# The first weights in eight transfers, two x tiles on ScalarE's queue, and another order at the end

## The chip, the cores and the metric

The kernel runs on one core of a Trainium2 chip. The metric is the time of one execution on the device in microseconds (us). The engines of the core are named as in the profile: PE is the matmul engine (TensorE), PEld its weight load, DVE is VectorE, ACT is ScalarE, POOL is GpSimd, SP is SyncE, which here only issues transfers (DMAs). Each engine works through its own instructions in the order in which they stand, and waits on semaphores for the others.

## What is computed

The input x is 2048 rows of 512 in bf16. The layer norm of it, xn, goes two ways, and the two meet at the end.

```python
def reference(A_x, A_wqkv, A_wo, B_x, B_w1, B_w2, B_w3, B_w4):
    x = A_x
    xn = _layernorm(x)
    s = _A_ref(xn, A_wqkv, A_wo)                      # 32 heads of 16, 8 keys at distance 2
    g = _silu(_B_ref(xn, B_w1, B_w2, B_w3, B_w4))     # mixer with shifts, then an MLP of 1376
    return x + s * g
# _A_ref: q, k, v = xn @ wqkv; each row i attends to rows i, i-2, .. i-14; softmax; o @ wo
# _B_ref: h = gelu(_layernorm(xn) @ w1); the four quarters of h are shifted by +1, -1, +2, -2 rows;
#         x1 = xn + h_shifted @ w2; x1 + gelu(_layernorm(x1) @ w3) @ w4
```

## The kernel before

Even and odd rows are kept apart (parity p = 0, 1), since attention at distance 2 never mixes them. Each parity is 1024 rows, held as eight tiles of 128 rows; four tiles are a chunk, so there are chunks 0 to 3. Rows lie on the partitions in the tiles `xn`, and the transposes `xnT` feed the projections.

**The start.** SP issues, in this order: x tiles 0 and 1 (128 KB each), the query half of the weights `wqk_sb` (512 KB in one transfer), x tiles 2 and 3, the key half, then the x tiles of chunks 1 and 2 in pairs, `w1_sb`, and chunk 3. Meanwhile PE runs ten warming matmuls on ones (`warm_ps`). For chunk 0, `stats` (DVE, L208 and L209) makes mean and variance of one tile, `root` (ACT, L217) the square root, `inverse` (DVE, L220) and `norm` (DVE, L224) the normalised tile. `first_columns` transposes tiles 0 and 1 on PE (L290) and copies the result out in halves, one on DVE (L292) and one on ACT (L293). Then `qk(0, 0)` projects these 256 rows: eight blocks `nt` of 128 output columns, of which 0 to 3 are queries and 4 to 7 keys, four matmuls each (L309). In front of blocks 6 and 7 PE transposes x tiles 2 and 3 (`columns`, L264, with DVE's copy at L270), which `qk(0, 1)` needs.

**The middle.** Mixer and MLP of the chunks follow (w1, w2, w3), and then 17 units of attention, n = 0 to 16, each with 120 queries of one parity (the first with 64 of each): `scores` (PE), `exps` (ACT, L627), `within` (DVE, L636, sets the weights outside the window to 0), `values` and `weighted` (PE, L663), with one tile of the last MLP matmul beside each (`w4_part`, L542, summed into x by DVE at L550). `weighted` returns the function that ACT runs to copy its result (L681). The units are grouped in 11 runs; runs 7, 8, 9 and 10 are the single units 13, 14, 15 and 16.

**The end.** The sums of the softmax of the last three runs are divided out on the chip: `sums_turn` transposes them (PE, L716), `sums_inverse` takes the reciprocal (DVE, L724) and spreads it to 16 columns per head (ACT, L729, two instructions), `rows` gathers the heads into `oT` (PE, L741, copied by ACT at L746), `sums_back` transposes the spread factors back (PE, L754) and `sums_mult` multiplies (DVE, L763). Run 7 is multiplied by POOL (`sums_apply`, L786) with factors that come through memory. `final(1, i)` multiplies tile i of parity 1 by wo (PE, L815). The function it returns, a gate, multiplies by silu of the other branch (DVE, L824 or L826) and adds x (POOL, L831). `store` writes the tiles out. The silu of tiles 14 and 15 is made by ACT at L560, for tile 15 out of PSUM, to which PE had added x by a matmul with the identity (L548).

The order on each engine is the order of the source: at its end the kernel chains every instruction to the one before it on the same engine.

Of the kernel before, what the change touches and what calls it, by code (L numbers as in the profile page):

```python
# [8 lines left out]
AF = mybir.ActivationFunctionType  # L9
ALU = mybir.AluOpType  # L10
# [5 lines left out]
def kernel(  # L16
# [14 lines left out]
    P = 128  # L31
# [80 lines left out]
    xn = [bigt([P, M // P, D], f"xn{p}") for p in range(2)]  # L112
    wqkv_v = A_wqkv.rearrange("(dt q) n -> q dt n", q=P)

    def load_x(c, n):
        p, k = c // 2, c % 2
        for t0 in range(k * TPC, (k + 1) * TPC, n):
            sp.dma_start(
                out=xn[p][:, t0 : t0 + n, :],
                in_=xv[p, t0 * P : (t0 + n) * P, :].rearrange("(i q) d -> q i d", q=P),  # L120
            )
            yield

    wqk_sb = midt([P, ND, 2 * D], "wqk_sb")
    first = load_x(0, 1)
    for k in range(2):
        next(first), next(first)
        sp.dma_start(out=wqk_sb[:, :, k * D : (k + 1) * D], in_=wqkv_v[:, :, k * D : (k + 1) * D])
    list(load_x(1, 2))
    list(load_x(2, 2))  # L130
    w1_sb = smt([P, ND, D], "w1_sb")
    sp.dma_start(out=w1_sb, in_=B_w1.rearrange("(dt q) n -> q dt n", q=P))
    list(load_x(3, 2))

    act.preload_act_table_set("sqrt_and_others")
    ident = const.tile([P, P], BF16, name="ident")
# [63 lines left out]
    def x_tile(c, j):  # L200
        return xn[c // 2][:, (c % 2) * TPC + j, :]

    def stats(c, j, key="l1"):
        if (key, c) not in mvs:
            mvs[key, c] = small.tile([P, TPC, nc.vector.BN_AGGR_DIM], F32, name=key + "m", tag=key + "m")
            rs[key, c] = small.tile([P, TPC], F32, name=key + "r", tag=key + "r")
        st = small.tile([P, nc.vector.BN_STATS_DIM], F32, name=key + "s", tag=key + "s")
        dve.bn_stats(out=st, in_=x_tile(c, j))  # L208
        dve.bn_aggr(out=mvs[key, c][:, j, :], in_=st)  # L209
# [6 lines left out]
    def root(c, a, b):  # L216
        act.activation(rs["l1", c][:, a:b], mvs["l1", c][:, a:b, 1], AF.Sqrt, bias=eps[:, 0:1])  # L217
# [211 lines left out]

    stats(0, 0)  # L430
    root(0, 0, 1)
    stats(0, 1)
    root(0, 1, 2)
    for j in range(2):
        inverse(0, j, j + 1)
        norm(0, j)
# [98 lines left out]
    def w4_part(t, lo, hi, tag="w"):  # L535
        c, jj = t // TPC, t % TPC
        if lo == 0:
            banks["w4", t] = pst(tag, "w4_ps")[:, 0, :]
        pt = banks["w4", t]
        for ft in range(lo, hi):  # L540
            fs = P if ft < NF - 1 else FL
            pe.matmul(  # L542
                pt, lhsT=h3[c][:fs, ft, jj * P : (jj + 1) * P], rhs=w4_sb[:fs, ft, :],
                start=(ft == 0), stop=(ft == NF - 1 and t < NN - 2),
            )
        x_i = x_tile(c, jj)
        if hi == NF and t == NN - 2:
            pe.matmul(pt, lhsT=ident[:], rhs=x_i, start=False, stop=True)  # L548
        elif hi == NF:
            dve.tensor_tensor(out=x_i, in0=pt, in1=x_i, op=ALU.add)  # L550
            gates.append(t)


    gates = []
    twice = set()

    def gate_silu(t):

        x_i = x_tile(t // TPC, t % TPC)
        act.activation(x_i, banks["w4", t] if t == NN - 2 else x_i, AF.Silu)  # L560
        twice.add(t)

    def gate_tanh():
# [152 lines left out]
            pe.matmul(pt[0:QU, g, :], lhsT=w[:, g, :], rhs=ident[:, DH::32], start=True, stop=True)  # L716
        rden[i] = pt

    def sums_inverse(i, copy=lambda: None, behind=False):

        pt = rden[i]
        rb = small.tile([P, 2 * ND, 4], BF16, name="rbt", tag="rbt")
        with nc.allow_low_precision("bf16 weights"):
            dve.reciprocal(out=rb[0:QU], in_=pt[0:QU])  # L724
        if not behind:
            copy()
        rx = slot().rearrange("p (s j c d) -> p s j c d", s=ND, j=2, c=4)
        for j in range(2):
            act.activation(  # L729
                rx[0:QU, :, j], rb[0:QU, j * ND : (j + 1) * ND, :].unsqueeze(3).to_broadcast([QU, ND, 4, DH]), AF.Copy  # L730
            )
        if behind:
            copy()
        rden[i] = rx

    def rows(i, tag):

        pt = pst(tag, "row_ps")[:, 0, 0 : ND * QU].rearrange("p (s q) -> p s q", s=ND)
        for dt in range(ND):
            for jj in range(2):  # L740
                pe.matmul(  # L741
                    pt[P // 2 * jj : P // 2 * (jj + 1), dt, :], lhsT=heads, rhs=orw[i][:, ND * jj + dt, :],
                    start=True, stop=True, tile_position=(0, P // 2 * jj),
                )
        _, _, _, q0, rw, parts = run_of(runs[i][0])
        return lambda: act.activation(oT[parts[0][0]][:, :, q0 : q0 + rw], pt, AF.Copy)  # L746

# [12 lines left out]
    def sums_mult(i):  # L760
        _, _, _, q0, rw, parts = run_of(runs[i][0])
        o = oT[parts[0][0]][:, :, q0 : q0 + rw]
        dve.tensor_tensor(out=o, in0=rden.pop(i), in1=o, op=ALU.mult)  # L763
# [92 lines left out]
    def store(q, p, i, n=2, cs=slice(0, D)):  # L856
        q.dma_start(
            out=ov[p, i * P : (i + n) * P, cs].rearrange("(i q) d -> q i d", q=P),
            in_=xo[p, i & ~1][:, i % 2 : i % 2 + n, cs],
        )  # L860
# [7 lines left out]
    for n in range(NN - 1):  # L868
        scores(n)
        back = [i for i, (a, b) in enumerate(runs) if b == n - 2 and i < R - NC]  # L870
        done = [i for i, (a, b) in enumerate(runs) if b == n - 1]
        evict = weighted(n - 1) if n > 0 else lambda: None
        for i in back:
            sums_invert(i)
        exps(n, 2 if n == 0 else 1)
        if n == NN - 2:
            values(n + 1)
        evict()
        if 0 < n < NN - 2:
            values(n + 1)  # L880
        gate_mult()
        if n < NN - 2:
            gate_tanh()
        for i in done:
            if i < R - NC:
                sums_gather(i)
        if n == 2:
            moves(0, [sp, pool], 1)
        for i in back:
            if 0 < i < R - NC - 1:  # L890
                moves(i, [sp], None, [6, 7])
            sums_read(i)
        for i in done:
            if i == 0:
                moves(i, [sp, pool], 0)
            elif i < R - NC - 1:
                moves(i, [pool, sp], None, range(6))
            elif i == R - NC - 1:
                moves(i, [pool], None, range(4))
            else:  # L900
                moves(i, [pool, sp])
        if n == NN - 2:
            store(sp, 0, 6)
        within(n, 2 if n == 0 else 1)
        late = [i for i, (a, b) in enumerate(runs) if n == max(b + 3, 5)]
        w4_part(n, 0, NF if n < NN - 2 else CUT)
        if n == 0:
            values(n + 1)
        gate = final(*final_at[n]) if n in final_at else None
        if n == NN - 2:  # L910
            banks["end"] = True
            sums_turn(R - 3, "o")
            sums_inverse(R - 3)
            for i in late:
                sums_apply(i)
        if gate:
            gate(pool)
        if n < NN - 2:
            for i in late:
                sums_apply(i)  # L920
        if n == NN - 3:
            moves(R - NC - 1, [pool], None, range(4, 8))
        if n % 2 == 0 and 10 <= n < NN - 3:
            load_xo((n - 2) // 8, (n - 2) % 8)
        if n - 1 in final_at and n % 2 == 0 and n < NN - 3:
            p, i = final_at[n - 1]
            store(sp, p, i - 1)
        if n in (10, 12):
            load_xo(1, n - 6)
    scores(NN - 1)  # L930
    evict = weighted(NN - 2)
    store(sp, 1, 0)
    exps(NN - 1)
    evict()
    act.preload_act_table_set("silu_and_others")
    w4_part(NN - 2, CUT, NF)
    gate_silu(NN - 2)
    within(NN - 1)
    gate2 = final(1, 2, "b")
    layout("high", f=1, g=1, h=1, i=1)  # L940
    sums_back(R - 3, "f")
    gate3 = final(1, 3, "h")
    sums_apply(R - 4, pool)
    evict = weighted(NN - 1, first=lambda: gate2(pool))
    evict()
    sums_turn(R - 2, "g")
    sums_inverse(R - 2, rows(R - 2, "i"), True)
    gate3(pool)
    store(sp, 1, 2)
    gate4 = final(1, 4, "w")  # L950
    sums_mult(R - 3)
    sums_turn(R - 1, "g")
    sums_back(R - 2, "f")
    sums_inverse(R - 1, rows(R - 1, "h"), True)
    sums_mult(R - 2)
    gate_silu(NN - 3)
    gate5 = final(1, 5, "b")
    gate4(pool)
    gate5(pool)
    store(sp, 1, 4)  # L960
    sums_back(R - 1, "i")
    gate6 = final(1, 6, "g")
    sums_mult(R - 1)
    halves = [slice(0, D // 2), slice(D // 2, D)]
    add6 = pe_add(1, 6, "o", slice(0, D))
    gate6(None)
# [48 lines left out]
```

## Time and profile before

| | us |
|---|---|
| time before, median of 3 runs (lowest to highest) | 198.19 (197.81 to 198.98) |
| the profiled execution's own time | 197.92 |
| its span, first to last instruction | 195.9 |
| warming matmuls on PE | 1.11 to 4.78 |
| first projection matmul on PE | 6.73 |
| last matmul ends | 192.3 |
| last transfer issued by SP and by ACT, end of issue | 193.36 and 193.29 |

The page gives the busy time of each engine as a share of the span. Its chain of work is followed back from the last instruction: at each step to what released it, or to the instruction before it on its engine. A timeline lists the instructions of one engine with start, length, what they read and write, and in brackets the idle time before them and what ended it. Times inside the span count from its start; 2.0 us lie around it in the profiled execution.

### The profile page before, as it was taken

How to read it: one execution, taken by the hardware profiler on the slowest of the kernel's cores; microseconds unless marked ns; L12 is line 12 of the kernel's file. 1: busy time of each engine (PE TensorE's matmuls, PEld its weight loads, DVE VectorE, ACT ScalarE, POOL GpSimd, SP SyncE). 2: the span in 40 equal slices, each digit the busy share in tenths (PEclk: the TensorE clock that was granted, in tenths of full speed). 3: DMA queues.
4: the chain of work that ended last, by engine and by line, in shares of the span. 5: the costliest groups of instructions: out<-in, count | busy, mean ns of one | idle time of the engine just before them, and what ended most of it. 6: DMA issues, size and time to landing. Idle time of an engine off the chain costs nothing.

```text
span 195.9 us, 6180 instructions
## 1 busy us (share of the span) xinstructions
PE 189.5 (97%) x2607; PEld 100.7 (51%) x2607; DVE 124.1 (63%) x247; ACT 126.7 (65%) x140; POOL 62.9 (32%) x114
## 2 busy tenths in 40 slices
PE   7799999999999999999999999999999999999992
PEld 2688748644444444444445555555555545546551
DVE  4879885029359968200005677788778888886893
ACT  3579867836721534666558788887666666677971
POOL 4146738201301121100000623032625242469761
PEclk9999999999999999999999999999999999999999
DMA  5985265799660366350420012222233271723243
GB/s 149 330 270 137 77 144 161 141 300 357 185 155 3 107 157 162 113 107 0 155 84 0 14 25 65 76 48 67 44 97 67 56 210 27 234 39 87 70 141 109
DMA packets 36251, 23.36 MB, mean 119 GB/s; under 512 B 19680, under 2 KB 35712, under 8 KB 36224
## 3 DMA queue, kind: packets, MB, share of 16 engines
q1 hardware_dynamic: 34864, 22.11, 40.2%
q0 software_dynamic: 1216, 0.81, 2.1%
q8 instruction: 20, 0.33, 0.7%
q10 hardware_dynamic: 144, 0.07, 0.1%
q14 instruction: 7, 0.06, 0.1%
HBM read 12.41 MB, written 5.36 MB: 91 GB/s over the span
## 4 chain that ended last, share of the span: by engine, by line
PE 90%; DVE 4%; ACT 2%; DMA 1%; issue 1%; DVEq 0%
PE w_ps L542 19%; PE w_ps L406 18%; PE qk_ps L309 14%; PE v_ps L595 8%; PE w_ps L342 7%; PE w_ps L366 7%; PE wo_ps L815 5%; PE o_ps L663 5%; PE s_ps L616 3%; PE w_ps L422 1%; DMA xn<-in_A_x_dram 1%; ACT prob L627 1%; DVE prob L636 1%; PE tr_ps L264 1%; PE dt_ps L716 1%
## 5 line engine op out<-in xcount | busy, mean ns | idle before, releaser
L627 ACT ACTIVATE prob<-s_ps 128x2048 bf16<-128x2048 f32 (+1 forms) x18 | 31.9, 1780 | 17.9 <-PE s_ps L616 17.9
L542 PE MATMUL w_ps<-w_sb,h3T 128*128 128x512 bf16 (+1 forms) x176 | 40.8, 380 | 0.0
L410 ACT ACTIVATE h3T<-w_ps 128x1024 bf16<-128x1024 f32 x20 | 20.5, 1023 | 24.9 <-PE w_ps L406 24.9
L706 POOL DMA_DIRECT2D oT<-orw x38 | 19.4, 518 | 49.8 <-DVE orw L671 30.3
L406 PE MATMUL w_ps<-x1nT,w_sb 128*128 128x512 bf16 x160 | 35.0, 379 | 0.0
L309 PE MATMUL qk_ps<-xnT,wqk_sb 128*128 128x256 bf16 (+1 forms) x224 | 29.7, 288 | 0.5 <-DVE xnT L292 0.4
L542 PEld LDWEIGHTS <-h3T 128*128 128x128 bf16 (+1 forms) x176 | 17.0, 98 | 20.4
L309 PEld LDWEIGHTS <-wqk_sb 128*128 128x128 bf16 x224 | 21.5, 98 | 7.6 <-issue 0.8
L406 PEld LDWEIGHTS <-w_sb 128*128 128x128 bf16 x160 | 15.6, 98 | 19.1 <-issue 0.4
L636 DVE TENSOR_TENSOR prob<-prob,band 128x2048 bf16<-128x2048 bf16 (+1 forms) x18 | 21.3, 1183 | 2.4 <-ACT prob L627 2.3
L316 ACT ACTIVATE qT<-qk_ps,sel 128x1024 bf16<-128x1024 f32 x16 | 16.8, 1111 | 7.1 <-PE qk_ps L309 7.0
L831 POOL TENSOR_TENSOR xo<-sg,xo 128x512 bf16<-128x512 bf16 x9 | 11.7, 1305 | 21.6 <-DVE sg L826 21.6
L371 DVE TENSOR_TENSOR xn<-w_ps,xn 128x1024 bf16<-128x1024 f32 x8 | 9.7, 1212 | 13.2 <-PE w_ps L366 13.2
L815 PE MATMUL wo_ps<-wo_sb,oT 128*128 128x512 bf16 (+1 forms) x68 | 16.6, 367 | 0.1
L595 PE MATMUL v_ps<-wv_sb,xnT 128*128 128x512 bf16 x64 | 16.6, 382 | 0.0
L550 DVE TENSOR_TENSOR xn<-w_ps,xn 128x512 bf16<-128x512 f32 x15 | 10.4, 690 | 7.5 <-PE w_ps L542 7.5
L598 DVE CAST v_aug<-v_ps 128x512 bf16<-128x512 f32 x1 | 0.7, 691 | 22.5 <-ACT h3T L410 22.5
L681 ACT ACTIVATE orw<-o_ps 128x896 bf16<-128x896 f32 x16 | 14.6, 913 | 0.4 <-PE dt_ps L716 0.4
L366 PE MATMUL w_ps<-w_sb,hT 128*128 128x512 bf16 x64 | 14.3, 379 | 0.0
L342 PE MATMUL w_ps<-xn2T,w_sb 128*128 128x512 bf16 x64 | 14.3, 379 | 0.0
L213 POOL TENSOR_SCALAR l3r<-l3m 128x4 f32<-128x4 f32 x4 | 1.8, 451 | 36.9 <-DVE l3m L209 36.9
L663 PE MATMUL o_ps<-prob,v_aug 64*32 64x64 bf16 x1088 | 12.2, 196 | 0.3 <-DVE prob L636 0.2
(100 smaller groups left out, 240.1 us busy)
## 6 DMA issues: line engine op xcount, KB each, us to landing
x1n_dram<-xn SPq DMA_DIRECT2D x4, 512.0 KB
xn<-in_A_x_dram SPq DMA_DIRECT2D x6, 256.0 KB
xo<-in_A_x_dram SPq DMA_DIRECT2D x6, 256.0 KB
out_dram<-xo SPq DMA_DIRECT2D x6, 256.0 KB
orw<-rden_d SPq DMA_DIRECT2D x6, 240.0 KB
w_sb<-in_B_w_dram SPq DMA_DIRECT2D x1, 1376.0 KB
w_sb<-in_B_w_dram SPq DMA_DIRECT2D x1, 1280.0 KB
wqk_sb<-in_A_wqkv_dram SPq DMA_DIRECT2D x2, 512.0 KB
```

Source lines behind the costliest of these rows:

```text
L309: pe.matmul(pt[:, b, :], lhsT=wqk_sb[:, dt, nt * P : (nt + 1) * P], rhs=xnT[p][:, dt, ms], start=(dt == 0), stop=(dt == ND - 1),)
L342: pe.matmul(pt[:, b, :], lhsT=w1_sb[:, dt, g * P : (g + 1) * P], rhs=xn2T[:, dt, :], start=(dt == 0), stop=(dt == ND - 1),)
L366: pe.matmul(pt[:, j, :], lhsT=w2_src(p, g, m0), rhs=w2_sb[:, g, :], start=(g == 0), stop=(g == ND - 1),)
L406: pe.matmul(pt[:, b, :], lhsT=w3_sb[:, dt, ft * P : (ft + 1) * P], rhs=x1nT[:, dt, :], start=(dt == 0), stop=(dt == ND - 1),)
L410: act.activation(h3_tile(c)[:, 2 * a : 2 * a + 2, :], pt, AF.Gelu_apprx_tanh)
L542: pe.matmul(pt, lhsT=h3[c][:fs, ft, jj * P : (jj + 1) * P], rhs=w4_sb[:fs, ft, :], start=(ft == 0), stop=(ft == NF - 1 and t < NN - 2),)
L595: pe.matmul(vp, lhsT=xnT[p][:, dt, k0 : k0 + P], rhs=wv_sb[:, dt, :], start=first, stop=last)
L627: act.activation(pr[:, rs_], t[:, rs_], AF.Exp, scale=SCALE)
L636: dve.tensor_tensor(out=w, in0=w, in1=b.unsqueeze(1).to_broadcast([P, m, KB]), op=ALU.min)
L663: pe.matmul(op[32 * cg : 32 * cg + 32, s, g * KB : (g + 1) * KB], lhsT=va[KB * s : KB * s + KB, dt * 8 + h, :], rhs=pr[KB * s : KB * s + K ...
L706: queues[hh % len(queues)].dma_start(out=oT[p][DH * hh : DH * (hh + 1), :, q0 : q0 + nq], in_=w[32 * cg : 32 * cg + DH, ND * jj : ND * jj ...
L815: pe.matmul(pt, lhsT=oT[p][:, dt, i * P : (i + 1) * P], rhs=wo_sb[:, dt, cs], start=(dt == 0), stop=(dt == ND - 1),)
```

## The change

1. The weights `wqk_sb` are loaded by eight transfers of 128 KB, one for each half and each 128 input rows, instead of two of 512 KB. All eight stand on SP's queue right behind x tiles 0 and 1.
2. x tiles 2 and 3 are issued by ACT instead of SP, one behind each of its first two roots.
3. At the end: the spread of run 8 goes behind the exponentials of unit 16, those of runs 9 and 10 are set apart from their reciprocals, the back-transposes of run 8 go behind `rows` of run 9, the add of tile 1 goes behind POOL's multiply for run 7, and gates, stores and multiplications stand in another order.
4. `rows` makes two matmuls of 480 columns instead of eight of 120.
5. x is added to the last MLP tile by DVE (`w4_add`), not by PE, and its silu reads SBUF and stands behind that of tile 14.

```diff
-    first = load_x(0, 1)
+    for j in range(2):
+        load_x(0, j)
     for k in range(2):
-        next(first), next(first)
-        sp.dma_start(out=wqk_sb[:, :, k * D : (k + 1) * D], in_=wqkv_v[:, :, k * D : (k + 1) * D])
-    list(load_x(1, 2))
-    list(load_x(2, 2))
+        for dt in range(ND):
+            sp.dma_start(out=wqk_sb[:, dt, k * D : (k + 1) * D], in_=wqkv_v[:, dt, k * D : (k + 1) * D])
+    for c in (1, 2):
+        for j in (0, 2):
+            load_x(c, j, 2)
...
     stats(0, 0)
     root(0, 0, 1)
+    load_x(0, 2, 1, act)
     stats(0, 1)
     root(0, 1, 2)
+    load_x(0, 3, 1, act)
...
     def rows(i, tag):
-        for dt in range(ND):
-            for jj in range(2):
-                pe.matmul(
-                    pt[P // 2 * jj : P // 2 * (jj + 1), dt, :], lhsT=heads, rhs=orw[i][:, ND * jj + dt, :],
+        for jj in range(2):
+            pe.matmul(
+                pt[P // 2 * jj : P // 2 * (jj + 1)], lhsT=heads, rhs=orw[i][:, ND * jj : ND * (jj + 1), :],
...
         if n == NN - 2:
             banks["end"] = True
             sums_turn(R - 3, "o")
-            sums_inverse(R - 3)
+            spread14 = sums_inverse(R - 3)
+            gate(None)
             for i in late:
                 sums_apply(i)
-        if gate:
+        elif gate:
             gate(pool)
...
     scores(NN - 1)
     evict = weighted(NN - 2)
-    store(sp, 1, 0)
     exps(NN - 1)
     evict()
+    spread14()
     act.preload_act_table_set("silu_and_others")
     w4_part(NN - 2, CUT, NF)
-    gate_silu(NN - 2)
     within(NN - 1)
+    w4_add(NN - 2)
     gate2 = final(1, 2, "b")
     layout("high", f=1, g=1, h=1, i=1)
-    sums_back(R - 3, "f")
     gate3 = final(1, 3, "h")
     sums_apply(R - 4, pool)
-    evict = weighted(NN - 1, first=lambda: gate2(pool))
+    gate.add(pool)
+    store(sp, 1, 0)
+    gate2(pool)
+    evict = weighted(NN - 1)
     evict()
     sums_turn(R - 2, "g")
-    sums_inverse(R - 2, rows(R - 2, "i"), True)
+    spread15 = sums_inverse(R - 2)
+    copy15 = rows(R - 2, "i")
+    sums_back(R - 3, "f")
     gate3(pool)
     store(sp, 1, 2)
+    spread15()
+    copy15()
     gate4 = final(1, 4, "w")
     sums_mult(R - 3)
+    gate4(pool)
     sums_turn(R - 1, "g")
     sums_back(R - 2, "f")
-    sums_inverse(R - 1, rows(R - 1, "h"), True)
+    spread16 = sums_inverse(R - 1)
+    copy16 = rows(R - 1, "h")
+    spread16()
+    copy16()
     sums_mult(R - 2)
     gate_silu(NN - 3)
+    gate_silu(NN - 2)
     gate5 = final(1, 5, "b")
-    gate4(pool)
     gate5(pool)
+    sums_back(R - 1, "i")
+    sums_mult(R - 1)
     store(sp, 1, 4)
-    sums_back(R - 1, "i")
     gate6 = final(1, 6, "g")
-    sums_mult(R - 1)
```

More of the change, by code (lines that the diff above doesn't have):

```diff
@@ L113, with load_x @@
     wqkv_v = A_wqkv.rearrange("(dt q) n -> q dt n", q=P)
[L115 to L122, printed above, removed]
+    def load_x(c, j, n=1, queue=sp):
+        p, t0 = c // 2, c % 2 * TPC + j
+        queue.dma_start(
+            out=xn[p][:, t0 : t0 + n, :], in_=xv[p, t0 * P : (t0 + n) * P, :].rearrange("(i q) d -> q i d", q=P)
+        )
     wqk_sb = midt([P, ND, 2 * D], "wqk_sb")
-    first = load_x(0, 1)
+    for j in range(2):
+        load_x(0, j)
     for k in range(2):
-        next(first), next(first)
-        sp.dma_start(out=wqk_sb[:, :, k * D : (k + 1) * D], in_=wqkv_v[:, :, k * D : (k + 1) * D])
-    list(load_x(1, 2))
-    list(load_x(2, 2))
+        for dt in range(ND):
[3 more added lines that the diff above has]
+            load_x(c, j, 2)
     w1_sb = smt([P, ND, D], "w1_sb")
     sp.dma_start(out=w1_sb, in_=B_w1.rearrange("(dt q) n -> q dt n", q=P))
-    list(load_x(3, 2))
+    for j in (0, 2):
+        load_x(3, j, 2)
     act.preload_act_table_set("sqrt_and_others")
@@ L543, in w4_part, with w4_add @@
                 pt, lhsT=h3[c][:fs, ft, jj * P : (jj + 1) * P], rhs=w4_sb[:fs, ft, :],
-                start=(ft == 0), stop=(ft == NF - 1 and t < NN - 2),
+                start=(ft == 0), stop=(ft == NF - 1),
             )
[L546 to L551, printed above, removed]
+        if hi == NF and t < NN - 2:
+            w4_add(t)
+    def w4_add(t):
+        x_i = x_tile(t // TPC, t % TPC)
+        dve.tensor_tensor(out=x_i, in0=banks.pop(("w4", t)), in1=x_i, op=ALU.add)
+        gates.append(t)
     gates = []
@@ L559, in gate_silu @@
         x_i = x_tile(t // TPC, t % TPC)
-        act.activation(x_i, banks["w4", t] if t == NN - 2 else x_i, AF.Silu)
+        act.activation(x_i, x_i, AF.Silu)
         twice.add(t)
@@ L717, in sums_turn, with sums_inverse @@
         rden[i] = pt
-    def sums_inverse(i, copy=lambda: None, behind=False):
+    def sums_inverse(i):
         pt = rden[i]
@@ L724, in sums_inverse, with spread @@
             dve.reciprocal(out=rb[0:QU], in_=pt[0:QU])
-        if not behind:
-            copy()
         rx = slot().rearrange("p (s j c d) -> p s j c d", s=ND, j=2, c=4)
[L728 to L733, printed above, removed]
-        rden[i] = rx
+        rden[i] = rx
+        def spread():
+            for j in range(2):
+                act.activation(
+                    rx[0:QU, :, j], rb[0:QU, j * ND : (j + 1) * ND, :].unsqueeze(3).to_broadcast([QU, ND, 4, DH]),
+                    AF.Copy,
+                )
+        return spread
     def rows(i, tag):
         pt = pst(tag, "row_ps")[:, 0, 0 : ND * QU].rearrange("p (s q) -> p s q", s=ND)
-        for dt in range(ND):
-            for jj in range(2):
-                pe.matmul(
-                    pt[P // 2 * jj : P // 2 * (jj + 1), dt, :], lhsT=heads, rhs=orw[i][:, ND * jj + dt, :],
-                    start=True, stop=True, tile_position=(0, P // 2 * jj),
-                )
+        for jj in range(2):
+            pe.matmul(
+                pt[P // 2 * jj : P // 2 * (jj + 1)], lhsT=heads, rhs=orw[i][:, ND * jj : ND * (jj + 1), :],
+                start=True, stop=True, tile_position=(0, P // 2 * jj),
+            )
         _, _, _, q0, rw, parts = run_of(runs[i][0])
```

## The prediction

> **What bounds the kernel now.** The page comes first: TensorE is busy in 97% of the span.
>
> ```profile
> span 195.9 us, 6180 instructions
> PE 189.5 (97%) x2607; PEld 100.7 (51%) x2607; DVE 124.1 (63%) x247; ACT 126.7 (65%) x140; POOL 62.9 (32%) x114
> ```
>
> So time can be won or lost only where PE is idle or serves another engine: before its first real matmul, and in the tail. Both parts of the change lie there. Second, the chain of work that ended last (start, length, what), its first pieces:
>
> ```profile
> 0.80 2.33 DMA xn<-in_A_x_dram
> 3.15 0.70 DVE l1s L208
> 4.06 0.59 DVE l1s L208
> 4.94 0.41 DVE xn L224
> 5.46 0.43 DVE xn L224
> 6.25 0.44 DVE xnT L292
> 6.73 2.94 PE qk_ps L309 x24
> ```
>
> The first x tile needs 2.33 us from issue to landing; then statistics, root, normalising and transposing of tiles 0 and 1 lead to the first projection at 6.73. From there PE runs nearly without a gap to 102 us, so each microsecond by which 6.73 moves is a microsecond of the total. The chain holds no weight transfer: the weights are not what it waits for. Third, ScalarE's timeline in this stage (start, length, what, idle time before it):
>
> ```profile
> 4.10 0.29 ACT L217 ACTIVATE l1r<-l1m,eps 128x1 f32<-128x1 f32 x1 [2.02 <-DVE l1m L209]
> 4.89 0.29 ACT L217 ACTIVATE l1r<-l1m,eps 128x1 f32<-128x1 f32 x1 [0.50 <-DVE l1r L220]
> 6.37 0.60 ACT L293 ACTIVATE xnT<-tr_ps 128x512 bf16<-128x512 bf16 x1 [1.18 <-PE tr_ps L290]
> ```
>
> The two roots stand on the chain, between 4.06 and 5.46. Fourth, the tail, from the timelines of ACT, DVE, POOL and SP's queue:
>
> ```profile
> 180.63 0.72 ACT L729 ACTIVATE slots<-rbt 120x256 bf16<-120x256 bf16 x2 [1.38 <-DVE rbt L724]
> 181.25 1.86 ACT L627 ACTIVATE prob<-s_ps 128x2048 bf16<-128x2048 f32 x1
> 183.14 1.68 DVE L636 TENSOR_TENSOR prob<-prob,band 128x2048 bf16<-128x2048 bf16 x1 [0.25 <-ACT prob L627]
> 184.28 1.49 POOL L786 TENSOR_TENSOR oT<-oT,orw 128x480 bf16<-128x480 bf16 x1 [0.54 <-DMA orw<-rden_d]
> 189.66 2.26 POOL L831 TENSOR_TENSOR slots<-slots 128x512 bf16<-128x512 bf16 x2 [1.40 <-PE wo_ps L815]
> 191.95 1.41 SPq L857 DMA_DIRECT2D out_dram<-slots  x3
> ```
>
> The last exponentials wait behind the two spreads of run 8 on ACT, and the last stores wait for POOL's two last adds, which end at 191.92.
>
> **The start, part by part.** SP issues one transfer each 0.48 us here ((3.69-0.80)/6). After the change its order is x0, x1 and eight weight rows w0 to w7, so w5 is issued at 0.80+7x0.48 = 4.2 and w6 at 4.65. x2 and x3 go to ACT, each behind a root. What decides is in the built program: the DMAs of SP and ACT share eight completion semaphores in turn, and a DMA waits on its issuing engine until the last user of its semaphore has landed. x2 takes the one of w5, x3 that of w6. That such a wait holds up the queue shows in SP's own waits (who, for what; us in total, times, longest):
>
> ```profile
> SPq L249 <- DMA wqk_sb<-in_A_wqkv_dram: 0.5, 1, 0.5
> ```
>
> L249 writes a row of factors and reads no weights. SP was free from 8.11 (6.50+1.61, its last loads) and stood still until about 8.6 for the second weight half.
>
> So on ACT the x2 issue cannot pass before w5 has landed, and queued behind it are root(0,1), the x3 issue and ACT's half of the first columns. DVE waits for that root with its inverse and normalising of tile 1, PE for the normalised tile. Landing of w5: by the row of x0, 4.2+2.33 = 6.5; by bytes, the table of half microseconds adds up to 1,070 KB by 6.0, and w5 ends at 1,049 KB, with 0.5 to 0.7 until the landing is seen (x0's 131 KB, about 2.5 to 3.1) again 6.5. Bounds: 5.9 (the 1.75 us that ACT's last store, issued at 192.90, took to its semaphore) and 6.9 (0.4 more for bytes that move slowly, as between 3.0 and 4.0 in that table). I take 6.45. Then the issue, 0.39 (ACT's store row), root(0,1) 0.29 and three gaps of 0.03 to 0.08: DVE's inverse starts at 7.27 instead of 5.26. That is +2.0 (1.4 to 2.5). The x3 issue finds w6 landed (7.0) and goes at 7.2; x3 lands at about 9.5, or 9.9 where it shares the 16 engines with SP's backlog. The columns of tiles 2 and 3 then have 0.3 us to spare: DVE's copy for qk(0,1) stands at 10.59 after an idle 0.32. I add 0.1 (0 to 0.5).
>
> The rest of the start costs nothing: six more issues on SP delay the later x loads by 1.9 us, but those stay ahead of PE, which is itself 2 us later. The key weights land at about 7.5 by x0's latency instead of about 8.6; nt 4 wanted them at 8.5, a gain of at most 0.2 that now lies under the larger delay.
>
> The backlog is what x3 has to pass, and no row here shows two queues loading at once. [...]
>
> **The tail, part by part.**
> - The spreads of run 8 go behind the last exponentials, which start when the scores end (180.60, not 181.35): -0.75. The masking after them took 1.68 while a POOL add ran, 1.21 in earlier turns; the add for tile 1 now comes later on POOL, so -0.45. It ends at 183.65 instead of 184.83.
> - PE drops the identity matmul (0.22) and moves run 8's four back-transposes (0.21) behind the last weighted sum, which starts at 184.1 instead of 184.87. PE is then the bound, no longer DVE.
> - DVE gains w4_add (0.69, row L550), hidden: masking 183.65, w4_add 184.3, gate2 184.9, then the last mix at 184.9, where PE has just delivered. ACT loses a Silu on PSUM (0.60) and gains one on SBUF (0.62), behind copy16.
> - rows() becomes 2 matmuls of 480 columns for 8 of 120: 0.33 before; 0.2 to 0.4. I take 0.3.
> - final(1,4) needs POOL's multiply for run 7, 184.28 to 185.77, whose transfer is not moved: start 185.8 instead of 186.42. Walking the waits from there: evict(16) on ACT ends at 186.3, spread15 186.9, run 9's back-transposes 187.3, recip(10) 187.8, spread16 188.55, sums_mult(10) 189.85, final(1,7) at 189.9 instead of 190.81. PE and DVE gain 0.9.
> - POOL does not: it now runs the multiply and then all five adds (1.15 each) in a row: 185.77+5x1.15 = 191.5, against 191.92. store(1,4) waits for that, and two more stores queue behind it at 0.47 each. So the end gains 0.4, up to 0.65 if POOL, now idle before its multiply, starts it as the transfer lands, and 0 if it slips. I take -0.45.
>
> **The sum, and TensorE's clock.** +2.1-0.45 = +1.65. The profiled execution took 197.92 (195.9 of span, 2.0 around it); the median is 198.19, 0.27 above. 198.19+1.65 = 199.85. One more thing hangs on the longer wait. Granted clock (PEclk) and PE's busy time (second number), in stretches of 3.41 us cut so that one ends where the clock falls:
>
> ```profile
> core 0: us, PE busy (x) PEld busy (x) DVE busy (x) ACT busy (x) POOL busy (x), PEclk, DMA share, GB/s
> ...
> 3.86:7.27 3.41, 2.26 (x17) 1.13 (x16) 2.90 (x9) 1.19 (x3) 0.00 (x0) 1.00 1.03 324
> ...
> 191.59:195.00 3.41, 0.70 (x6) 0.29 (x3) 1.01 (x3) 0.87 (x2) 0.33 (x1) 1.00 0.47 154
> 195.00:195.90 0.90, 0.00 (x0) 0.00 (x0) 0.00 (x0) 0.00 (x0) 0.00 (x0) 0.50 0.03 9
> ```
>
> After a stretch with 0.70 us of PE work the clock fell to half, 2.7 us after the last matmul. After the change PE has, between the warm-up's end at 4.78 and the first projection at 8.8, only eight transposes (0.92 by their row): a hole of 4 us, with 2 us empty in its middle. Before it was 2 us. At its first matmuls the slow state lasted 2.75 us (seven of warm_ps at 620 ns, the last at 379). A relapse costs half of that, 1.4, less what falls before the projections: 0.7 to 1.7, taken as 1.2. Then 199.85+1.2 = 201.05.
>
> [...]
>
> **The rivals.**
> 1. The clock relapses (forecast, 201.05). For it: the hole is longer than the 2.7 us at the end. Against: the transposes inside it, and only one fall in the trace to judge by. Chance 0.5.
> 2. ACT blocks, the clock holds: 199.85. Chance 0.35.
> 3. Not slower: w5 lands early enough. The place is ACT's x2 issue. Each microsecond of earlier landing takes one off; to break even with the tail, root(0,1) may start at most 0.45 later than 4.89, so w5 must be in by 4.9, 0.7 us after its issue. With no wait at all and the tail's 0.45 it gives 197.75; with the full 0.9 in the tail 197.3. x0's 2.33 speaks against it. With landings at 5.9 and the tail's 0.9 it is 198.8, still within the bound below. Chance of all this 0.11.
> 4. x3 comes late too (behind SP's 2 MB backlog, by 1 us) with a relapse: 202.1. Chance 0.04.
>
> **Numbers.** About 0.5% (1.0 us) is what a measurement of this kernel can tell from no change. Faster than 197.2 needs rival 3 and more: 0.03. Within 0.5%, up to 199.2: most of rival 3 and the low edge of 2, 0.12. Slower: 0.85. The range runs from 199.2 (rival 2 with w5 at 6.0 and 0.65 from the tail) to 202.0 (forecast with the longest relapse and late x3).
>
> **What would show it.** ACT's second L217 at about 6.9 behind an ACT-queue DMA; first qk_ps at 8.8; a PEclk of 0.5 between 7 and 13 us and qk_ps matmuls well above the page's mean for that form there for the forecast, none of it for rival 2; last exponentials at 180.6 plus the start's delay; POOL's last five adds without gaps into the last stores. It is wrong if the second root starts before 6, or if final(1,7) is not 0.7 us earlier against the first projection.

## The result, and the profile after

The changed kernel takes 204.85 us (median of 6 runs, 203.40 to 206.11) against 198.29 (197.81 to 198.98) for the kernel before on the same chip: a ratio of 1.0313, with a 95% interval of 1.0271 to 1.0356. It is slower, as forecast, but by 6.6 us and not by 2.9, and 2.85 us above the upper end of the range. The profiled execution took 203.97. A ratio is taken over the runs within 1.5% of a kernel's fastest; for one experiment below (`end_period`) these are three of twelve, and there the single times are read.

The page of the changed kernel, beside the one shown of before (span 195.9, PE busy 189.5):

```profile
span 202.1 us, 6139 instructions
PE 190.6 (94%) x2569; PEld 101.7 (50%) x2594; DVE 124.3 (61%) x248; ACT 126.4 (63%) x140; POOL 62.4 (31%) x114
PEclk9969999999999999999999999999999999999999
```

The span grew by 6.2 us and PE's busy time by 1.1, so 5.1 us are new idle time of PE. The 6 in the third slice is a piece at half clock. The chain of work that ended last begins so (start, length, what):

```profile
4.09 2.95 DMA wqk_sb<-in_A_wqkv_dram
7.06 5.28 DMA xn<-in_A_x_dram
12.36 0.70 DVE l1s L208
```

Before, the chain held x tile 0 and the arithmetic. Now it begins with a weight transfer (w5) and then x tile 2, which lasts 5.28 us from issue to landing, where x tile 0 took 2.33. ScalarE's timeline shows the first link, PE's the result:

```profile
4.01 0.29 ACT L217 ACTIVATE l1r<-l1m,eps 128x1 f32<-128x1 f32 x1 [1.94 <-DVE l1m L209]
7.06 0.39 ACTq L117 DMA_DIRECT2D xn<-in_A_x_dram  x1
7.49 0.29 ACT L217 ACTIVATE l1r<-l1m,eps 128x1 f32<-128x1 f32 x1 [3.18 <-DMA wqk_sb<-in_A_wqkv_dram]
7.57 0.36 ACTq L117 DMA_DIRECT2D xn<-in_A_x_dram  x1
```

```profile
9.29 4.51 PE L309 MATMUL qk_ps<-xnT,wqk_sb 128*128 128x256 bf16 x24 [0.40 <-DMA xn<-in_A_x_dram]
14.71 0.40 PE L264 MATMUL tr_ps<-ident,xn 128*128 128x128 bf16 x4 [0.91 <-DVE xn L224]
```

The transposes of tile 2 in PE's timeline before:

```profile
9.51 0.39 PE L264 MATMUL tr_ps<-ident,xn 128*128 128x128 bf16 x4
```

The second root waits 3.18 us behind the issue of x2 (7.06), which waits for w5 (landed at 7.04). The first projection starts at 9.29 instead of 6.73, and the transposes of tile 2 at 14.71 instead of 9.51: 5.2 us of the 6.2 are lost by here. The windows of the clock, cut where it falls and returns (columns as in the prediction, PEclk after the five engines):

```profile
6.61:10.02 3.41, 1.13 (x11) 0.87 (x12) 1.00 (x3) 0.89 (x2) 0.00 (x0) 1.00 0.73 220
10.02:13.43 3.41, 3.41 (x19) 2.41 (x17) 1.03 (x3) 0.12 (x1) 0.00 (x0) 0.50 0.92 305
```

The other loss is at the end. DVE's timeline there, then POOL's (L numbers are those of the kernel shown, two or more lines off from before):

```profile
191.34 0.63 DVE L828 TENSOR_TENSOR slots<-wo_ps,xn 128x512 bf16<-128x512 f32 x1
193.40 0.66 DVE L765 TENSOR_TENSOR oT<-rr_ps,oT 128x480 bf16<-128x480 f32 x1 [1.44 <-DMA oT<-orw]
```

```profile
190.82 3.37 POOL L833 TENSOR_TENSOR xo<-slots,xo 128x512 bf16<-128x512 bf16 x3
194.73 1.15 POOL L833 TENSOR_TENSOR slots<-slots 128x512 bf16<-128x512 bf16 x1 [0.53 <-DVE slots L828]
196.58 1.15 POOL L833 TENSOR_TENSOR slots<-slots 128x512 bf16<-128x512 bf16 x1 [0.70 <-DVE slots L828]
```

DVE's multiplication of run 8 waits 1.44 us for a move of run 8 into `oT`. Before, it waited for nothing:

```profile
186.95 0.65 DVE L763 TENSOR_TENSOR oT<-rr_ps,oT 128x480 bf16<-128x480 f32 x1
```

From the start of the weighted sum of unit 15 to the start of the last matmul of the kernel it takes 12.14 us (186.23 to 198.37), before 11.37 (180.65 to 192.02). I call this stretch the tail; it grew by 0.8 where I expected it to shrink.

### The profile page after: what moved, and what is told of

The parts are those of the page before. It is cut to its first block, busy times and chain, and to the rows that moved or that the text cites. A ratio compares the mean times of both kernels' runs of the same rounds, so it can differ in the third digit from the quotient of the medians.

```text
span 202.1 us, 6139 instructions
## 1 busy us (share of the span) xinstructions
PE 190.6 (94%) x2569; PEld 101.7 (50%) x2594; DVE 124.3 (61%) x248; ACT 126.4 (63%) x140; POOL 62.4 (31%) x114
## 3 DMA queue, kind: packets, MB, share of 16 engines
HBM read 12.41 MB, written 5.36 MB: 88 GB/s over the span
## 4 chain that ended last, share of the span: by engine, by line
PE 73%; DMA 11%; SPq 4%; ACT 3%; DVE 3%; issue 2%; POOL 1%; DVEq 0%; ACTq 0%
PE w_ps L406 17%; PE w_ps L544 13%; PE qk_ps L309 12%; DMA oT<-orw 7%; PE w_ps L366 7%; PE w_ps L342 7%; PE v_ps L597 6%; PE wo_ps L817 4%; PE o_ps L665 3%; DMA xn<-in_A_x_dram 3%; PE s_ps L618 2%; ACT orw L683 2%; DMA wqk_sb<-in_A_wqkv_dram 1%; SPq L694 1%; PE w_ps L422 1%
## 5 line engine op out<-in xcount | busy, mean ns | idle before, releaser
L309 PE MATMUL qk_ps<-xnT,wqk_sb 128*128 128x256 bf16 (+1 forms) x223 | 31.2, 298 | 0.6 <-DMA xn<-in_A_x_dram 0.4
L309 PEld LDWEIGHTS <-wqk_sb 128*128 128x128 bf16 x224 | 22.4, 101 | 8.3 <-DMA xn<-in_A_x_dram 0.5
L597 PE MATMUL v_ps<-wv_sb,xnT 128*128 128x512 bf16 x49 | 15.8, 383 | 0.8
L553 DVE TENSOR_TENSOR xn<-w_ps,xn 128x512 bf16<-128x512 f32 x16 | 11.0, 690 | 8.2 <-PE w_ps L544 8.1
L208 DVE BATCH_NORM_STATS2 l1s<-xn 128x6 f32<-128x512 bf16 x16 | 10.8, 673 | 4.5 <-DMA xn<-in_A_x_dram 4.5
```

The source lines that it names most:

```text
L309: pe.matmul(pt[:, b, :], lhsT=wqk_sb[:, dt, nt * P : (nt + 1) * P], rhs=xnT[p][:, dt, ms], start=(dt == 0), stop=(dt == ND - 1),)
L597: pe.matmul(vp, lhsT=xnT[p][:, dt, k0 : k0 + P], rhs=wv_sb[:, dt, :], start=first, stop=last)
```

## The experiments on the start

**The two halves of the change.** `start_only` has the changed loads and the old end, `end_only` the old loads and the changed end. Both take the one hunk of the diff and leave the other.

> The start of the changed kernel with the end of the kernel before. In the changed kernel's profile everything after the start stands about 5.3 us later than before, and the tail lost about 1 us more. Theory: the start alone costs 5.3 us, so 203.5 us, with x tile 2 landing about 5 us after its issue on ScalarE's queue. Rival: half of the loss comes from the new end, by way of the order of transfers, so about 201.

> The start of the kernel before with the end of the changed kernel. Theory: PE is 0.8 us earlier at the end, so that a 16 KB fetch of instructions (queue q8) takes one DMA engine while run 8's last move is on its way; its last sixteenth lands 1.9 us late and DVE's multiplication at L763 waits 1.4 us for it: about 1 us slower than before, 199.2. Rival (the prediction's sum): POOL's five adds in a row set the end, 0.45 us faster, 197.8.

`start_only`: 205.37 us (203.90 to 207.09, 4 runs), ratio 1.0349 [1.0308, 1.0390], above the 203.5 that I expected. `end_only`: 199.72 (197.56 to 201.56, 12 runs), ratio 1.0056 [1.0020, 1.0091]. So the loads alone make the loss, and the new end alone does not gain what I counted on but loses about 1 us by the ratio (1.6 by the medians of all runs), in two groups of runs: two at 197.6, ten from 199.4 on. Of the profiled run of `end_only`, 200.17, 1.8 us come from the start, where the second weight half landed at 10.4 instead of 8.6 by unchanged code; the end is therefore read by the length of its tail. In the profile of `start_only` ScalarE issues x2 at 7.01, but x3 only at 9.04: its issue waits for w6, which landed at 9.02 there and at 7.55 in the changed kernel. x3 lands at 15.22 (13.22), and since DVE's statistics of tile 3 stand ahead of the normalising of tile 2, PE transposes tile 2 at 16.71 (14.71). The clock is at half from 9.50 to 12.91, and again from 16.33, after this longer hole. Among the six runs of the changed kernel, two have a mean granted clock of 0.99 and took 203.4 and 204.0; the four with 0.982 or 0.983, a second such stretch by that figure, took 204.2 to 206.1, 1.6 us more in the mean. How much of that is the clock and how much a late x3, these runs do not tell.

**Eight weight transfers without ScalarE's queue.** `eight_sp` keeps the eight transfers, but SP issues x2 and x3, between the two halves of the weights.

```diff
     for k in range(2):
+        for j in (2, 3) if k else ():
+            load_x(0, j)
         for dt in range(ND):
-    load_x(0, 2, 1, act)
-    load_x(0, 3, 1, act)
```

> The kernel before with the weights in eight transfers and x tiles 2 and 3 left on SP's queue between the two halves. Theory: the wait on ScalarE and the backlog ahead of x tile 2 are the cause, the eight transfers are not: within 0.6 us of before, with tile 3 landing at about 6.5. Rival: eight transfers move slowly (the changed kernel's DMA ran at 200 to 250 GB/s where before it ran at 350), so tiles 2 and 3 land 2 us later and the kernel is 1 to 2 us slower.

198.81 us (198.51 to 199.15, 8 runs), ratio 1.0034 [1.0014, 1.0055]. Splitting the weights costs 0.7 us (0.3 to 1.1), a little more than the 0.6 that I allowed; x3 landed at 7.74 and not at 6.5. The loss lies with the two x tiles on ScalarE's queue.

**The wait and the place in the queue.** Three kernels change when x2 is issued and what SP has issued by then. In all three SP's later loads (chunks 1 to 3 and `w1_sb`) stand behind ScalarE's two x tiles in the source. The trace of the changed kernel has eight completion semaphores for the transfers of SP and ACT, used in turn in the order of the built program: x2 is the 16th transfer there and has that of w5, which landed at 7.04. In these three it is the 11th and has that of w0, which landed at 4.39 in the changed kernel; it was issued at 4.56 in `hold` and at 4.68 in `lane_free`. `hold` lets SP's later loads wait for the normalised tile 1; `lane_free` lets them wait only for mean and variance of tile 1; `hold_wait` is `hold`, and ScalarE reads a column of w5 ahead of x2 and one of w6 ahead of x3, so that its issue waits as in the changed kernel.

```diff
 # hold: the later loads of SP, moved behind the normalising of tiles 0 and 1
+    sp.dma_start(out=row_dram[3:4, :], in_=xn[0][0:1, 1, :])
+    for c in (1, 2):
+        for j in (0, 2):
+            load_x(c, j, 2)
 # lane_free: the later loads moved behind the two roots, and
-    sp.dma_start(out=row_dram[3:4, :], in_=xn[0][0:1, 1, :])
+    sp.dma_start(out=mark_dram, in_=mvs["l1", 0][0:1, 1, :])
 # hold_wait: hold, and
+    act.activation(seen[:, 0:1], wqk_sb[:, 1, D : D + 1], AF.Copy)
     load_x(0, 2, 1, act)
+    act.activation(seen[:, 1:2], wqk_sb[:, 2, D : D + 1], AF.Copy)
     load_x(0, 3, 1, act)
```

> The changed start, but SP's loads of chunks 1 to 3 and of w1 stand behind a small SP transfer that waits until tile 1 is normalised, so nothing is queued behind the weights; in this order x tiles 2 and 3 also take completion semaphores that are free early (weights 0 and 1), so ScalarE does not wait either. Old end. Theory (wait and backlog): tile 2 is issued at 4.4 and lands at about 6.7, tile 3 at 7.5; first projection at 6.8; within 0.6 us of before, up to 1 us slower if chunk 1 comes late. Rival (ScalarE's queue itself is slow): tile 2 lands 5 us after its issue, and the kernel is 2 us slower.

> The changed start with the old end, but ScalarE doesn't wait: x2's transfer shares its completion semaphore with the first weight piece and x3's with the third, so both leave right behind the two roots at about 4.4 and 5.0 us. SyncE's 2 MB of later loads stay directly behind the weights. Theory A (two things are needed: ScalarE is held to 7.06, and only then does x2 stand behind loads that SyncE issued in between): x2 is ahead of those loads and lands by 8.8, as in the run with the loads held back; PE's transposes of tile 2 at about 10.7 to 11.2, time 199.2 to 200.0. Theory B (a second queue is served late whenever SyncE's queue is full, whenever it was issued): x2 lands at 11 or later, transposes of tile 2 at 13 or later, time 201.5 to 204.

> The run with SyncE's later loads held back, in which ScalarE now waits for weight pieces 5 and 6 ahead of x2 and x3, by reading a column of each piece. Leaves out nothing. Theory A (the wait moves only the issue; with an idle queue x2 needs 2.5 to 3.5 us from issue): x2 issued at 7.0, landed at 9.5 to 10.5, second root and x3 correspondingly later; 1.2 to 2.2 us above the run without the wait, 200.6 to 201.6, and up to 1.7 more if the clock falls back: 203. Theory C (the wait alone makes the whole loss): as the changed start, 204.5 to 206. Theory B (the backlog alone makes it): as without the wait, 199.4 within 0.5.

The timelines of ACT and of PE in `lane_free`:

```profile
4.68 0.38 ACTq L118 DMA_DIRECT2D xn<-in_A_x_dram  x1
5.11 0.29 ACT L211 ACTIVATE l1r<-l1m,eps 128x1 f32<-128x1 f32 x1 [0.87 <-DVE l1r L214]
```

```profile
10.81 0.40 PE L258 MATMUL tr_ps<-ident,xn 128*128 128x128 bf16 x4 [0.85 <-DVE xn L218]
```

and the same two in `hold_wait`:

```profile
6.97 0.38 ACTq L117 DMA_DIRECT2D xn<-in_A_x_dram  x1
7.40 0.29 ACT L210 ACTIVATE l1r<-l1m,eps 128x1 f32<-128x1 f32 x1 [0.23 <-issue]
```

```profile
9.30 3.86 PE L302 MATMUL qk_ps<-xnT,wqk_sb 128*128 128x256 bf16 x24 [0.30 <-DVE xnT L285]
13.00 0.39 PE L257 MATMUL tr_ps<-ident,xn 128*128 128x128 bf16 x4
```

All six kernels in one table; the fourth column is the first packet of ScalarE's queue in the DMA records, and the landing is the completion of x2 there.

| kernel | SP's later loads issued from | x2 issued | its first packet | x2 landed | tile 2 on PE | time (ratio to before) |
|---|---|---|---|---|---|---|
| before | | 2.2 (SP) | | 6.10 | 9.51 | 198.1 to 198.6 |
| `hold` | 6.30 | 4.56 | 5.74 | 8.41 | 10.71 | 199.39 (1.0076 [1.0051, 1.0101]) |
| `lane_free` | 6.14 | 4.68 | 6.46 | 8.53 | 10.81 | 199.44 (1.0057 [1.0028, 1.0085]) |
| `hold_wait` | 8.71 | 6.97 | 8.08 | 9.21 | 13.00 | 202.84 (1.0222 [1.0177, 1.0268]) |
| changed | 5.51 | 7.06 | 10.06 | 12.34 | 14.71 | 204.85 (1.0313 [1.0271, 1.0356]) |
| `start_only` | 5.51 | 7.01 | 9.97 | 12.41 | 16.71 | 205.37 (1.0349 [1.0308, 1.0390]) |

`hold` was meant to take the backlog away; it only moved it 0.8 us, which was enough. Its x2 landed at 8.41 and not at 6.7, and it took 1.5 us more than the kernel before, where I had allowed 1. What the table sorts by is the order of issue. Where x2 is issued ahead of SP's later loads, it lands 2.2 to 3.9 us after its issue. Where SP has issued four loads of 256 KB in the 1.5 us before it, with the last weights still under way, x2's first packet moves only 3.0 us after the issue and it lands after 5.3 to 5.4. The order is not kept to the end: in the changed kernel both queues move packets from 10.06 on, and the last two of SP's four loads land behind x2, at 12.89 and 13.74. Loads that SP issued behind x2 did not make it as late (`lane_free`, 199.4: loads from 6.14 on, x2 in at 8.53, 3.85 us after its issue; the second of those loads left at 7.46, when its own semaphore came free). A backlog ahead of x2 without the wait was not run. The wait alone costs about 3 us against `hold` (1.5% by the two ratios), more than the 1.2 to 2.2 that I gave it without a fall of the clock and within what I gave it with one: x2 landed 2.2 us after its issue, but PE starts the first projection 2.4 us later (9.30 for 6.90), and its 24 matmuls took 3.86 us, where they took 2.94 before, since a part of them ran at half clock (8.13 to 11.55). Wait and backlog together (`start_only`) cost 5.4 us against `hold` (2.7%). What inside the DMA engines serves the queues in this order, no run here tells.

## The experiments on the end

**Earlier moves.** In `end_only` the same multiplication waits for the same move:

```profile
189.65 0.66 DVE L763 TENSOR_TENSOR oT<-rr_ps,oT 128x480 bf16<-128x480 f32 x1 [1.52 <-DMA oT<-orw]
```

Its tail takes 12.17 us. In the traces each of SP's moves sends 16 updates to its semaphore, here called its parts, and it counts as landed with the last; of this move 15 came by 187.88 and the last at 189.24. Just then, from 187.21 to 188.14, a packet of 16,384 bytes ran on a queue that carries nothing else: 20 such packets in the span, each taking 0.9 to 1.4 us in the changed kernel and 0.9 to 1.8 before. From the start of one to the start of the next the changed kernel has 104 to 209 matmuls, 128 in the mean. The page has the queue (packets, MB, share of 16 engines):

```profile
q8 instruction: 20, 0.33, 0.7%
```

I read it as the fetch of PE's code: the page calls the queue `instruction`, and 20 packets of 16,384 bytes over the 2569 matmuls and 2594 weight loads on the changed kernel's page are 63 bytes for each. PE's matmuls run on through the fetch at 187.21; the move that it meets comes late. The thirteen profiles together say the same: of the moves into `oT` during whose flight such a packet ran (between the issue and the landing of the 15th part), 273 of 561 have their last part over 0.8 us behind the 15th, and of the others 13 of 366. `end_moves` and `end_split` issue SP's moves of run 8 ahead of the read of run 7's factors, all four and two of the four:

```diff
 # end_split; at unit 15
+        if n == NN - 2:
+            moves(R - NC, [pool, sp], None, range(4))
         for i in back:
             sums_read(i)
...
-                moves(i, [pool, sp])
+                moves(i, [pool, sp], None, range(4, 8))
```

> The old start with the changed end, and at tile 14 SyncE issues run 8's moves ahead of the read-back of run 7 instead of behind it, so that they leave about 1.5 to 3 us earlier. Theory A (the late landing of run 8's last part is what the changed end lost; it was late because PE, running 0.8 us earlier, fetched its code while the moves were under way): DVE's copy waits for no landing, the tail is as forecast, and the time is 197.4 to 198.0, 0.2 to 0.8 below the kernel before. Theory D (the changed end is slower for another reason, DVE or POOL at the very end): 199.2 to 200.2, as the changed end alone (199.72). Rival to both: the read-back of run 7, now later, holds POOL's multiplications, and the last additions of POOL end the kernel 0.5 to 1 us later than in A: 198.2 to 198.8.

> The old start with the changed end; at tile 14 SyncE issues two of its four moves of run 8 ahead of the read-back of run 7 and two behind it. SyncE stood idle there for 3 us (180.1 to 183.3 in the run of the changed end alone) until run 7's reciprocals were stored, so the two moves go early and the read leaves no later. Theory A (what the changed end lost is the late landing of SyncE's moves of run 8): neither DVE's multiplication of run 8 waits for a landing nor PE for POOL's multiplication of run 7, and the time is 0.2 to 0.8 below the kernel before: 197.4 to 198.2. Theory D (the end is bounded by DVE and POOL behind it): as the changed end alone, 199.2 to 200.2.

`end_moves`: 200.33 (199.13 to 202.05, 6 runs), ratio 1.0105 [1.0056, 1.0154]. DVE no longer waits for the move, but the rival came true and at a higher price: SP's read of run 7 left late, POOL's multiplication with it, and PE stood before `final(1, 4)`:

```profile
187.81 1.04 PE L815 MATMUL wo_ps<-wo_sb,oT 128*128 128x512 bf16 x3 [1.08 <-POOL oT L786]
```

The tail takes 11.98. `end_split`: 197.59 (197.07 to 200.19, 12 runs), ratio 0.9957 [0.9930, 0.9983]. Neither wait is there, in the timelines of PE, DVE and POOL:

```profile
186.57 1.03 PE L815 MATMUL wo_ps<-wo_sb,oT 128*128 128x512 bf16 x3
```

```profile
186.95 0.64 DVE L763 TENSOR_TENSOR oT<-rr_ps,oT 128x480 bf16<-128x480 f32 x1
```

```profile
186.25 3.39 POOL L831 TENSOR_TENSOR xo<-slots,xo 128x512 bf16<-128x512 bf16 x3
189.58 2.28 POOL L831 TENSOR_TENSOR slots<-slots 128x512 bf16<-128x512 bf16 x2
```

The tail takes 10.73 (181.35 to 192.08), and POOL's five adds run without a gap. This is the changed end as it was forecast.

**The fetch itself.** `end_fetch` leaves the changed end as it is and moves the fetches: 112 tiny matmuls replace four of the ten warm-up matmuls. `end_period` has 132, which is 20 more, and with them PE executes 128 matmuls more than in `end_only`, the mean distance of two fetches above. `before_fetch` is the kernel before with the 112.

```diff
-    for i in range(10):
+    for i in range(6):
         pe.matmul(wm[:, i % 2, :], lhsT=ones_bf[:], ...)
+    for i in range(112):       # 132 in end_period
+        k, c, g = i % 2, i // 2 % 4, i // 8 % 8
+        pe.matmul(
+            wm[32 * c : 32 * c + 32, k, 64 * g : 64 * g + 64],
+            lhsT=ones_bf[64 * k : 64 * k + 64, 0:32], rhs=ones_bf[64 * k : 64 * k + 64, 0:64],
+            start=True, stop=True, tile_position=(64 * k, 32 * c),
+        )
```

> The old start with the changed end; of PE's ten warm-up matmuls four are replaced by 112 tiny ones, which changes nothing but the places at which PE's code is fetched: the fetch of 16 KB that fell into the moves of run 8 (187.21 us) comes some 100 matmuls earlier, at about 182.5, and the next at about 190. Theory A1 (the fetch on one of the 16 DMA engines makes the last part of run 8's move late): that part lands with the others, by about 187.8, DVE's multiplication of run 8 starts by 188.3 instead of 189.65 against a start as in that run, and the time is 197.6 to 198.6. Theory A2 (the part is late without the fetch, by the queues or the engine itself): it stays 1 us or more behind the others and the time is 199.2 to 200.2. The warm-up also holds the clock: if the tiny matmuls do not, the first projection runs at half clock and 1.2 to 1.7 us are lost ahead of tile 2; the tail is then to be read against the first projection.

> The run with the tiny warm-up matmuls on the old start and the changed end, with 132 of them in place of 112, so that PE executes 128 matmuls (256 instructions with their weight loads, 16 KB at 64 bytes each) more than with the changed end alone: one whole period of the code fetches. Nothing else is different from that run. Theory A1 (the place of the fetch decides): the fetches are back where they were with the changed end alone, one starts 4.6 to 4.9 us after the beginning of the weighted sum of unit 15, the last part of a move of run 8 lands more than 1 us behind the other 15, DVE's multiplication of run 8 waits 1 us or more, from that weighted sum to the last matmul it takes 11.9 to 12.3 us (10.73 with 112), and the time is 199 to 200. Theory A3 (it was not the fetch; the other warm-up or chance made that run fast): 10.7 to 10.9 us there, and 197.5 within 0.5.

> The kernel before, with the same 112 tiny warm-up matmuls for four of the ten, and nothing else. Theory A1 (the moves of run 8 just escape the fetch in the kernel before, and escape it here): the tail takes 11.1 to 11.5 us from the weighted sum of unit 15 to the last matmul as before (11.37), and the time is 197.6 to 198.6. Theory A3 (the tiny warm-up itself is worth the 1 us that it brought on the changed end): 197.0 to 197.5.

| kernel | time, median (12 runs) | runs below 199 | fetch | the move DVE needs: 15 parts, last part | tail |
|---|---|---|---|---|---|
| before (profiled run) | 198.1 to 198.6 | | 185.83 to 187.64 | 185.86, 185.87 | 11.37 |
| changed (6 runs) | 204.85 | | 190.81 to 192.22 | 191.39, 193.28 | 12.14 |
| `end_only` | 199.72 | 2 | 187.21 to 188.14 | 187.88, 189.24 | 12.17 |
| `end_split` | 197.59 | 10 | 186.25 to 187.30 | 185.43, 185.44 | 10.73 |
| `end_fetch` | 197.50 | 11 | 185.80 to 186.76 | 184.74, 184.75 | 10.73 |
| `end_period` | 200.07 | 3 | 186.27 to 187.64 | 186.39, 186.40 | 10.84 |
| `before_fetch` | 198.09 | 9 | 187.16 to 188.12 | 186.01, 186.02 | 11.10 |

`end_fetch` is 0.9940 [0.9912, 0.9968] of the kernel before. The time came as expected (197.6 to 198.6; 197.50), the place of the fetch did not: 112 matmuls for four are 108 more, nearly the mean distance of two fetches (128), so the fetch fell 0.8 us later against the weighted sum of unit 15 (5.55 us behind its start, `end_only` 4.76), and not 100 matmuls earlier. Also SP's read and moves left 0.9 us earlier against that point, which this run does not separate from the fetch. The clock held through the tiny warm-up: the first 16 projection matmuls took 1.97 us, where 24 took 2.94 before. With 20 tiny matmuls more in the warm-up (`end_period`) and the fetch back near its place (4.85 us behind that start in the profiled run), nine of twelve runs take 200.0 to 201.7, four of them at a granted clock of 0.999 or 1.0. Its profiled run, 197.81, is one of the three others: the fetch came at 186.27 and the move's last part at 186.40, a race won by a hair. So the expected 11.9 to 12.3 of the tail was not seen there. The times of the nine fit it, but none of them has a profile; part of their loss may lie elsewhere, as at the start, where in the profiled run the second weight half landed at 9.53 (8.59 in `end_fetch`). `before_fetch` (ratio 1.0005 [0.9975, 1.0034]) shows that the tiny warm-up itself brings nothing. By the profiles of `end_only` and of the changed kernel, the new end loses because PE reaches the fetch 0.4 to 0.6 us earlier (4.76 us behind the start of that weighted sum in `end_only`, 4.58 in the changed kernel, 5.18 before), while the move is in as late as before (5.43, 5.16 and 5.22 for the last part that no fetch held up).

## Why the prediction was wrong

The direction and the first link were right. Step by step, by the profiled execution:

- **ACT's x2 issue waits for w5: +2.0 (1.4 to 2.5).** Right in kind; w5 landed at 7.04, outside my bounds of 5.9 to 6.9; the loads came in at 250 GB/s on average between 3 and 8 us, where the kernel before moved 292. The second root started at 7.49 (forecast 6.9), the first projection at 9.29 (8.8): +2.56.
- **x2 and x3 behind SP's backlog: "I add 0.1 (0 to 0.5)".** This is the step that failed. I let x3 land 2.3 us after its issue (7.2 to 9.5) and x2 ahead of it; x2 took 5.28, x3 5.65 (7.57 to 13.22), and the start lost another 2.64 us by it (5.20 less 2.56). I had priced the backlog as shared bandwidth from the start; instead no packet of x2 moved until 10.06, while SP's loads did, and only then the queues shared. The kernel before held a nearer row than that of x0: its own x2, issued at 2.2 behind the first weight half, landed at 6.10, 3.9 us later. From the issue of x2 to its first packet it took 3.0 us, where `hold_wait`, without the backlog, has 1.1. Rival 4 named this mechanism and gave it 1 us and a chance of 0.04.
- **The clock, +1.2.** The relapse came, from 10.02 to 13.43, after a window with 1.13 us of PE work. It cost nothing in this execution, since PE then waited for tile 2 until 14.71 all the same: here the term does not add to the step above, it lies under it. The clock was back at 1.00 after a window in which PE was busy for 3.41 us of 3.41.
- **The middle, 0.** +0.4: the weighted sum of unit 15 stands 5.58 later, tile 2 5.20. No run looked into that.
- **The tail, -0.45.** +0.8 here, -0.6 in `end_split` and `end_fetch`. The sub-steps up to the race held, against the delay of 5.58: last exponentials at 186.30 (forecast 186.18), masking in 1.23 (1.21), `weighted(16)` at 189.75 (189.68), `final(1, 4)` at 191.45 (191.38). The step that failed is `sums_mult` of run 8, which I let follow PE and DVE alone. I did not walk SP's moves of run 8, on which it also waits; they kept their old time while everything around them came earlier, and the fetch then met them.

Put together, 2.56 + 2.64 + 0.38 + 0.77 = 6.35 us of PE's time; the span grew by 6.2. The prediction's own sign of being wrong is there: `final(1, 7)` starts 187.83 us behind the first projection, 184.08 before, and not 0.7 us earlier. One slip in the working carries no weight: SP has four more issues ahead of its later loads, not six, since x2 and x3 left its queue; the delay was 1.8 us (5.51 for 3.69) against the 1.9 I gave.

Two versions beat the kernel before, both with the old start and the changed end: `end_split`, with two moves ahead of the read (by 0.4%), and `end_fetch`, with the other warm-up (by 0.6%).

## What to carry to other kernels

Here x2 was issued at 7.06 on the second queue, behind w5, where it left at 2.2 on the first: before moving a load to another queue, look up which semaphore its issue waits for, and what the other queue has issued by then. A change that makes the compute engines earlier must be walked through the transfers too: in `end_only` PE came to the fetch 0.4 us earlier than before, and the move of run 8 came no earlier (15 parts in by 5.43 us behind the start of the weighted sum of unit 15, before by 5.21). Where run times of one kernel fall into two groups, look for two things that meet, and read more than one profile.

## What was new of the hardware

- With four loads of 256 KB issued on SP's queue in the 1.5 us before x2, ScalarE's first packet moved 3.0 us after its issue (changed kernel and `start_only`), and 1.1 to 1.8 us after it where the issue was ahead of those loads (`hold_wait`, `hold`, `lane_free`).
- Where a packet of 16,384 bytes on the instruction queue, by my reading a fetch of PE's code, ran beside a move, the last of the move's 16 parts came 1.4 us behind the 15th in `end_only` and 1.9 us in the changed kernel. With 20 tiny matmuls more in the warm-up, 180 us earlier, the median stood 2.6 us higher (200.07 for 197.50); they shift where the fetches fall, but the runs behind that median have no profile.
